# A recurrent attention kernel whose TensorE products are widened to 128 rows, and whose carry sum moves from VectorE to TensorE and ScalarE

## The chip, the cores and the metric

The kernel runs on one core of a Trainium2 chip. The core has five engines that run side by side, each with an instruction queue of its own that it works through in order: TensorE (PE in the profile, with its weight loads shown apart as PEld), VectorE (DVE), ScalarE (ACT), GpSimd (POOL) and SyncE (SP), which here only issues transfers. The metric is device time in microseconds (us) of one execution; lower is better. Three runs of the kernel before gave 1849.24, 1849.33 and 1851.26 us, a median of 1849.33 us.

## The reference

The computation has two parts. The first is a recurrence over 768 time steps for 4 batches of 8 heads, with a 40 x 40 state for each head:

```python
for t in range(S):
    kt, vt, rt = (k[:, :, t], v[:, :, t], r[:, :, t])
    wt, at, bt = (w[:, :, t], a[:, :, t], b[:, :, t])
    y[:, :, t] = np.einsum('bhd,bhde->bhe', rt, state)
    Sa = np.einsum('bhde,bhe->bhd', state, at)
    state_decay = state * wt[:, :, None, :] - np.einsum('bhd,bhe->bhde', Sa, bt)
    state = state_decay + np.einsum('bhd,bhe->bhde', vt, kt)
```

The second takes the 3072 x 320 output of the first as `x` and runs eight experts over it, `relu(x @ w1[e]) @ w2[e]` with 1024 hidden columns each, summed with gate weights `P` that come from `x @ w_gate` by an exponential and eight rounds of row and column normalisation. Everything is float32.

## The kernel before

**The recurrence in chunks.** `attention` cuts the 768 steps into 12 chunks of 64 steps (`NCH`, index `c`) and treats each of the 4 batches (`b`) as one unit, so there are 48 units (c, b). The 8 heads of a batch are held as 4 pairs (`NP`); a pair takes partitions 0 to 39 and 64 to 103, so that many tiles have 104 partitions (`R2`), the rows between being zero. All products of this part are float32; each call of `matmul` shows in the trace as two MATMUL instructions, each transpose as one.

**Preparation.** `prep(c, b)` (lines 106 to 169) needs only the inputs. It loads them, runs two scans on DVE (lines 113 and 123), scales the inputs (`kb` and `ab`, lines 137 to 144, on POOL for most units), multiplies them (`ll`, line 149, a 104-row product) and transposes `kb` (`kt`, line 157). Parts of the results go into the unit's `sx` and `bb` tiles by ScalarE copies (lines 145, 146, 164 to 166). A triangular inverse is needed for each chunk. It is made for two chunks at a time (`GROUPS`) on DVE by `inv_diag`, `contract` and `inv_off` (lines 171 to 198), and `tmat` (lines 223 to 237) finishes it with two sets of 64-row products, `gp` (line 230) and `op` (line 235).

**The recurrence of one unit.** `recur` (lines 239 to 312) is a chain over four engines:

1. `av` (line 259, TensorE, 104 rows) into PSUM, multiplied by a mask into `f` by DVE (line 260).
2. `xc[0]` and `xc[1]` (line 267, TensorE, 104 rows); ScalarE copies their upper part to `x1` (line 273) and their lower part to `c1` (line 274).
3. `pu` (line 278, TensorE, 128 rows, 104 columns for each pair), multiplied by a mask into `pm` by DVE (line 280).
4. `c2` (line 285, TensorE, 128 rows); DVE adds `c1` to it and writes `ws` (line 287).
5. POOL makes the output `y` (line 291) and then the carry `z` (line 302; DVE does it from chunk 9 on); TensorE transposes `z` (line 307) and ScalarE copies it (lines 309 and 310) for the unit of the same batch in the next chunk.

The PSUM tiles `av`, `xc`, `pu`, `c2` and `zt` share four buffers (tag `ps`). `f`, `rb` and `x1` are tiles of rotating pools; `vz` and `c1` are fixed buffers that are cleared once in `clear` (lines 81 to 87). `gate` (line 317) adds a product with 8 columns for each pair.

**Order.** An event list (lines 355 to 391) gives the order in which the units' steps are written down; the four batches are staggered by `SKEW`, and the preparation of chunk 2 and later and the inverses are interleaved with the recurrence. A list scheduler that works with a model of durations then fixes the order of instructions on each engine. From `N_MAN` = 8 blocks of the second part on, the order is the written one.

**The experts.** `body` (from line 439) runs the second part with products of 320 and 384 columns (lines 620 and 555) in the type `fp32r`, one MATMUL for each call. Its weights' preparation and its first blocks are mixed with the last chunks of the recurrence.

Of the kernel before, what the change touches and what calls it, by code (L numbers as in the profile page):

```python
# [29 lines left out]
def attention(ctx, tc, d, xd, ps, pq, pt, gs, lg):  # L30
    nc = tc.nc
    pin = ctx.enter_context(tc.tile_pool(name="a_in", bufs=1))
    inv = ctx.enter_context(tc.tile_pool(name="a_inv", bufs=1))
    sets = [ctx.enter_context(tc.tile_pool(name=f"a_set{i}", bufs=1)) for i in range(NSX)]
    const = ctx.enter_context(tc.tile_pool(name="a_const", bufs=1))
    io = ctx.enter_context(tc.tile_pool(name="a_io", bufs=1))
    wk = ctx.enter_context(tc.tile_pool(name="a_wk", bufs=2))
# [14 lines left out]
    for n in range(NCH * NB - NSX, NCH * NB):  # L52
        i, pool = n % NSX, sets[n - NCH * NB + NSX]
        if i in IN_SETS or i in KB_SETS:
            raw = pool.tile([128, 1252], F32, name=f"st{i}")
            raws[i] = raw
            sx_b[i] = raw[0:R2, 0:832].rearrange("r (p h x) -> r p h x", h=2, x=104)
            bb_b[i] = raw[:, 832:1248].rearrange("r (p x) -> r p x", x=104)
            cc_b[i] = raw[0:R2, 1248:1252]
            continue  # L60
        sx_b[i] = pool.tile([R2, NP, 2, 104], F32, name=f"sx{i}")
# [28 lines left out]
    def first_use(i):  # L90
        if i in fresh:
            fresh.discard(i)
            nc.gpsimd.memset(bb_b[i], 0.0)
            nc.scalar.copy(out=sx_b[i][64:R2].rearrange("r p h x -> r (p h) x")[:, :, 64:104],
                           in_=cst[64:R2, 360:400].unsqueeze(1).broadcast_to([40, 8, 40]))

    state = {"sx": 0, "ab": 0, "g1": 0, "vz": 0, "c1": 0, "t1": 0, "tt": 0}

    def rot(key, lst):
        i = state[key]  # L100
# [5 lines left out]
    def prep(c, b, ld):  # L106
# [38 lines left out]
        nc.scalar.copy(out=sx[64:104, :, 0, 0:64], in_=ab[0:40, :, 0:64])  # L145
        nc.scalar.copy(out=sx[64:104, :, 1, 0:64], in_=ab[64:104, :, 64:128])
        ll = pq.tile([128, NP, 2, 64], F32, name="ll", tag="pq")
        for p in range(NP):
            nc.tensor.matmul(ll[:, p], lhsT=kb[:, p], rhs=ab[:, p], start=True, stop=True)  # L149
        if cb < NKB:  # L150
            nc.scalar.activation(out=lt, in_=ll[64:128], func=AF.Copy, scale=-1.0)
            (nc.sync if cb < N_SP else nc.scalar).dma_start(out=ld[GRP[c][1], :, b], in_=lt)
# [2 lines left out]
            kt = pq.tile([128, NP, 2, 64], F32, name="kt", tag="pq")  # L155
        for p in range(NP):
            nc.tensor.transpose(kt[:, p].rearrange("s h x -> s (h x)")[:, 0:R2],
                                kb[:, p].rearrange("r k s -> r (k s)"), ident[0:R2, 0:R2])
# [43 lines left out]
    def tload(c):  # L202
        tt = rot("tt", tt_b)
        tts[c] = tt
        ld, ud, nd = invs[GRP[c][0]]
        t1, t2, lb = td_b[0][0:64], td_b[0][64:128], lg_b[0][0:64]
        cc = GRP[c][1]
        q = [slice(h * 32, h * 32 + 32) for h in range(2)]
        u = [[slice(cc * 64 + blk * 32 + h * 16, cc * 64 + blk * 32 + h * 16 + 16) for h in range(2)]
             for blk in range(2)]  # L210
        for h in range(2):
            nc.sync.dma_start(out=lb[q[h], :, q[h]],
                              in_=ld[cc, 0:32].rearrange("j b p h s -> j (b p) h s")[:, :, h, 32:64])
        for h in range(2):
            nc.sync.dma_start(out=t1[q[h]], in_=nd[u[0][h]].rearrange("g j s -> j g s"))
        for h in range(2):
            nc.sync.dma_start(out=t2[q[h]], in_=ud[u[1][h]].rearrange("g j s -> j g s"))
        for h in range(2):
            for blk in range(2):
                r = slice(h * 64 + blk * 32, h * 64 + blk * 32 + 32)  # L220
                nc.sync.dma_start(out=tt[r, :, r], in_=ud[u[blk][h]].rearrange("g j s -> j g s"))

    def tmat(c, half):
        gl = slice(half * 8, half * 8 + 8)
        tt = tts[c][:, gl]
        t1, t2 = td_b[0][0:64, gl], td_b[0][64:128, gl]
        lb, gs = lg_b[0][0:64, gl], lg_b[0][64:128, gl]
        gp = pt.tile([64, 2 * NP, 32], F32, name="gp", tag="pt")
        for p in range(2 * NP):
            nc.tensor.matmul(gp[:, p], lhsT=lb[:, p], rhs=t1[:, p], start=True, stop=True)  # L230
        nc.scalar.copy(out=gs[0:32, :, 0:32], in_=gp[0:32])
        nc.scalar.copy(out=gs[32:64, :, 32:64], in_=gp[32:64])
        op = pt.tile([64, 2 * NP, 32], F32, name="op", tag="pt")
        for p in range(2 * NP):
            nc.tensor.matmul(op[:, p], lhsT=gs[:, p], rhs=t2[:, p], start=True, stop=True)
        nc.scalar.copy(out=tt[0:32, :, 32:64], in_=op[0:32])
        nc.scalar.copy(out=tt[64:96, :, 96:128], in_=op[32:64])

    def recur(c, b):
        pp = preps[c, b]  # L240
        vz, zc = vz_cur[b], zp[b]
        nc.sync.dma_start(out=vz[:, :, 0:64], in_=d["v"][c, b])
        vz = vz[0:R2]
        rb = io.tile([RP, NP, 128], F32, name="rb", bufs=NRB)
        nc.sync.dma_start(out=rb, in_=d["r"][c, b])
        rb = rb[0:R2]
# [11 lines left out]
        for p in range(NP):  # L258
            nc.tensor.matmul(av[:, p], lhsT=vz[:, p], rhs=rb[:, p], start=True, stop=True)  # L259
        nc.vector.tensor_tensor(  # L260
            out=f[:, :, :, 0:64], in0=av,
            in1=mask_f.unsqueeze(1).unsqueeze(1).broadcast_to([R2, NP, 2, 64]), op=ALU.mult)
        yield
        xc = [ps.tile([R2, NP, 104], F32, name=f"xc{h}", tag="ps") for h in range(2)]
        for h in range(2):
            for p in range(NP):
                nc.tensor.matmul(xc[h][:, p], lhsT=pp["sx"][:, p, h], rhs=f[:, p, h], start=True, stop=True)  # L267
                if p % 2:
                    gate_step()
        x1 = wk.tile([128, NP, 104], F32, name="x1")  # L270
        c1 = rot("c1", c1_b)
        for h in range(2):
            nc.scalar.copy(out=x1[h * 64:h * 64 + 64], in_=xc[h][0:64])
            nc.scalar.copy(out=c1[h * 64:h * 64 + 40], in_=xc[h][64:104])
        yield
        pu = ps.tile([128, NP, 104], F32, name="pu", tag="ps")
        for p in range(NP):
            nc.tensor.matmul(pu[:, p], lhsT=tts[c][:, b * NP + p], rhs=x1[:, p], start=True, stop=True)  # L278
        pm = wk.tile([128, NP, 104], F32, name="pm")
        nc.vector.tensor_tensor(out=pm, in0=pu, in1=mask_p.unsqueeze(1).broadcast_to([128, NP, 104]),  # L280
                                op=ALU.mult)
        yield
        c2 = ps.tile([R2, NP, 104], F32, name="c2", tag="ps")
        for p in range(NP):
            nc.tensor.matmul(c2[:, p], lhsT=pp["bb"][:, p], rhs=pm[:, p], start=True, stop=True)  # L285
        ws = wk.tile([R2, NP, 104], F32, name="ws")
        nc.vector.tensor_tensor(out=ws, in0=c2, in1=c1, op=ALU.add)  # L287
# [523 lines left out]
```

## Time and profile before

| quantity | value |
|---|---|
| median of three runs | 1849.33 us (1849.24 to 1851.26) |
| the profiled execution | 1847.82 us |
| its span, first to last instruction | 1846.0 us |
| granted TensorE clock, mean over the span | 0.954 |
| ACT busy | 855.9 us (46%) |
| POOL busy | 873.1 us (47%) |
| SP: transfers of the input tile `inp` | 42, 450.2 KB each |

Durations in the text come from the one profiled execution, which took 1.8 us more than its span. "Busy" for PE is the time in which at least one MATMUL was under way. As these are pipelined, a product's duration in the trace (some 255 ns) is longer than the distance at which products follow each other. "PEclk" or "clock" is the share of the full TensorE clock that was granted. The chain of waits follows the work that ended last back from the end of the program, at each step to what released it. It gives shares of time by engine and line, and "issue" in it is time in which the engine waited for nothing that the profile shows.

### The profile page before, as it was taken

How to read it: one execution, taken by the hardware profiler on the slowest of the kernel's cores; microseconds unless marked ns; L12 is line 12 of the kernel's file. 1: busy time of each engine (PE TensorE's matmuls, PEld its weight loads, DVE VectorE, ACT ScalarE, POOL GpSimd, SP SyncE). 2: the span in 40 equal slices, each digit the busy share in tenths (PEclk: the TensorE clock that was granted, in tenths of full speed). 3: DMA queues.
4: the chain of work that ended last, by engine and by line, in shares of the span. 5: the costliest groups of instructions: out<-in, count | busy, mean ns of one | idle time of the engine just before them, and what ended most of it. 6: DMA issues, size and time to landing. Idle time of an engine off the chain costs nothing.

```text
span 1846.0 us, 31552 instructions
## 1 busy us (share of the span) xinstructions
PE 1734.9 (94%) x11843; PEld 1705.9 (92%) x11843; DVE 1397.2 (76%) x2306; ACT 855.9 (46%) x1848; POOL 873.1 (47%) x848
## 2 busy tenths in 40 slices
PE   5479898999989999999999999999999999999999
PEld 4378788899888999999999999999999999999999
DVE  7877969768698768677786868977686877778675
ACT  6347666666643534344343443445343443435342
POOL 6535556441572618355371826006291744628170
PEclk8569988889899999999999999999999999999999
DMA  8467787875720102011110202201020111102001
GB/s 211 116 152 177 184 183 181 182 173 133 203 82 31 56 1 75 20 56 38 38 56 19 75 20 67 65 14 57 19 75 19 57 38 38 57 19 75 5 34 43
DMA packets 194957, 145.10 MB, mean 79 GB/s; under 512 B 143861, under 2 KB 171637, under 8 KB 194805
## 3 DMA queue, kind: packets, MB, share of 16 engines
q1 hardware_dynamic: 191125, 137.35, 28.3%
q10 hardware_dynamic: 3680, 5.74, 1.1%
q8 instruction: 94, 1.54, 0.4%
q14 instruction: 58, 0.48, 0.1%
HBM read 117.00 MB, written 26.04 MB: 77 GB/s over the span
## 4 chain that ended last, share of the span: by engine, by line
PE 76%; DVE 10%; DMA 6%; issue 4%; ACT 2%; POOL 2%; SPq 1%; DVEq 0%; ACTq 0%; POOLq 0%
PE op L620 36%; PE p L555 33%; DMA inp<-in_inp_dram 2%; PE xc L267 2%; DVE pr L183 2%; DVE gt L186 1%; PE pu L278 1%; DVE q L113 1%; PE c L285 1%; PE av L259 1%; DVE un L186 1%; DMA ld<-lt 1%; DVE gf L123 1%; DMA rb<-in_r_dram 1%; DVE hl L579 1%
## 5 line engine op out<-in xcount | busy, mean ns | idle before, releaser
L555 PE MATMUL p<-xch,wh 128*128 128x384 f32 (+1 forms) x1792 | 605.7, 339 | 9.2 <-DVE sm L573 5.6
L576 ACT ACTIVATE hh<-sm 128x384 fp32r<-128x384 f32 x512 | 269.4, 526 | 726.4 <-DVE sm L573 726.2
L620 PE MATMUL op<-wh,hh 128*128 128x320 f32 x1536 | 476.8, 311 | 1.0 <-ACT hh L576 0.9
L620 PE MATMUL op<-wl,hh 128*128 128x320 f32 x1536 | 474.6, 309 | 0.0
L620 PE MATMUL op<-wh,hl 128*128 128x320 f32 x1536 | 467.1, 309 | 0.7 <-DVE hl L579 0.7
L501 POOL TENSOR_TENSOR wl<-ws,wh 128x640 fp32r<-128x640 f32 x60 | 103.6, 1727 | 608.5 <-ACT wh L499 608.3
L579 DVE SCALAR_TENSOR_TENSOR hl<-sm,hh 128x384 fp32r<-128x384 f32 x512 | 375.6, 767 | 2.4 <-ACT hh L576 2.0
L555 PEld LDWEIGHTS p<-xch,wh 128*128 128x128 f32 (+1 forms) x1792 | 337.4, 188 | 13.4 <-DVE sm L573 6.8
L555 PE MATMUL p<-xcl,wh 128*128 128x384 f32 x896 | 302.5, 338 | 0.0
L555 PE MATMUL p<-xch,wl 128*128 128x384 f32 x896 | 301.8, 337 | 0.0
L620 PEld LDWEIGHTS op<-wh,hh 128*128 128x128 f32 x1536 | 290.2, 189 | 1.6 <-ACT hh L576 1.5
L620 PEld LDWEIGHTS op<-wl,hh 128*128 128x128 f32 x1536 | 291.0, 189 | 0.0
L620 PEld LDWEIGHTS op<-wh,hl 128*128 128x128 f32 x1536 | 286.9, 188 | 1.1 <-DVE hl L579 0.9
L573 DVE TENSOR_TENSOR sm<-p,u 128x384 f32<-128x384 f32 x384 | 234.3, 621 | 8.8
L555 PEld LDWEIGHTS p<-xcl,wh 128*128 128x128 f32 x896 | 168.7, 188 | 0.0
L555 PEld LDWEIGHTS p<-xch,wl 128*128 128x128 f32 x896 | 168.6, 188 | 0.0
L573 DVE TENSOR_TENSOR sm<-p,p 128x384 f32<-128x384 f32 x128 | 71.2, 557 | 128.5 <-PE p L555 76.5
L573 DVE TENSOR_TENSOR p<-p,p 128x384 f32<-128x384 f32 x128 | 71.1, 555 | 98.7 <-PE p L555 98.0
L573 DVE TENSOR_TENSOR u<-p,p 128x384 f32<-128x384 f32 x128 | 70.8, 553 | 59.7 <-PE p L555 58.6
L509 POOL TENSOR_TENSOR wl<-ss,wh 128x512 fp32r<-128x512 f32 x60 | 89.9, 1498 | 32.7 <-ACT wh L506 28.4
L149 PE MATMUL ll<-ab,kb 104*128 104x128 f32 x336 | 64.0, 350 | 43.8 <-POOL ab L144 22.2
L291 POOL TENSOR_TENSOR y<-ws,gr 104x256 f32<-104x256 f32 x48 | 49.5, 1031 | 117.3 <-DVE ws L287 95.0
(156 smaller groups left out, 2774.4 us busy)
## 6 DMA issues: line engine op xcount, KB each, us to landing
ws<-in_wts_dram SPq DMA_DIRECT2D x60, 832.0 KB
inp<-in_inp_dram SPq DMA_DIRECT2D x42, 450.2 KB
rb<-in_r_dram SPq DMA_DIRECT2D x48, 224.0 KB
gd<-gf SPq DMA_DIRECT2D x48, 113.8 KB
gr<-gd SPq DMA_DIRECT2D x48, 113.8 KB
vz<-in_v_dram SPq DMA_DIRECT2D x48, 112.0 KB
ld<-lt ACTq DMA_DIRECT2D x40, 128.0 KB
f<-in_vt_dram SPq DMA_DIRECT2D x48, 80.0 KB
```

Source lines behind the costliest of these rows:

```text
L149: nc.tensor.matmul(ll[:, p], lhsT=kb[:, p], rhs=ab[:, p], start=True, stop=True)
L183: nc.vector.tensor_tensor(out=prv, in0=a.unsqueeze(3).broadcast_to([nu, n_c, n_k, n_r]), in1=m.unsqueeze(1).broadcast_to([nu, n_c, n_k, n_ ...
L186: nc.vector.tensor_reduce(out=dst, in_=prv.rearrange("u c k r -> u c r k"), op=ALU.add, axis=AX.X)
L267: nc.tensor.matmul(xc[h][:, p], lhsT=pp["sx"][:, p, h], rhs=f[:, p, h], start=True, stop=True)
L291: nc.gpsimd.tensor_tensor(out=y[:, :, b % 2], in0=ws[:, :, 0:64], in1=gr[0:R2, :, 64:0:-1], op=ALU.mult)
L501: g.tensor_tensor(out=wl[:, 0:640], in0=raw[:, 256:896], in1=wh[:, 0:640], op=ALU.subtract)
L509: g.tensor_tensor(out=lv[:, 3:7], in0=so[:, :, 0], in1=hv[:, 3:7, 0], op=ALU.subtract)
L555: nc.tensor.matmul(o, lhsT=w_, rhs=x_, start=(j == 0), stop=(j == 3))
L573: eng.tensor_tensor(out=out, in0=x, in1=y, op=ALU.add)
L576: nc.scalar.activation(out=hh[:, f, h], in_=sm[f][:, h], func=AF.Relu)
L579: v.scalar_tensor_tensor(out=hl[:, f, h], in0=sm[f][:, h], scalar=0.0, in1=hh[:, f, h], op0=ALU.max, op1=ALU.subtract)
L620: nc.tensor.matmul(ops[i], lhsT=a[:, h, cs], rhs=w_[:, cw], start=(f == 0 and h == 0 and j == 0), stop=(last and h == 1 and j == 2))
```

## The change

Two things are changed. First, products whose operands have 104 rows get operands with 128 rows: `sx`, `ab`, `kb`, `f`, `rb`, `vz` and `c1` become tiles of 128 partitions, of which the added rows are zero. `f`, `rb` and `x1` become fixed buffers that rotate, so that their zeros stay; new ScalarE instructions (`zero`) write these once. Products whose rows number 128 or 64 anyway get more columns instead: `pu` takes 128 columns for each pair in place of 104, and `gp` and `op` take 64 in place of 32, the second half of which is overwritten by the next product of the loop. `kt`, `zt` and the gate's products stay as they are, and so do the `ll` products of the first six units, whose `kb` lies in another tile.

Second, for chunks 0 to 7 (`CI` = 8) the sum of `c1` and `c2` is formed in PSUM. One more product, of the identity with `c1` (128 rows, 416 columns), starts the accumulation group, the four `bb` products add to it, and ScalarE copies the result to `ws`. From chunk 8 on DVE adds as before.

```diff
-            sx_b[i] = raw[0:R2, 0:832].rearrange("r (p h x) -> r p h x", h=2, x=104)
+            sx_b[i] = raw[:, 0:832].rearrange("r (p h x) -> r p h x", h=2, x=104)
...
-    td_b = [const.tile([128, 4 * NP, 32], F32, name="td")]
+    td_b = [const.tile([128, 4 * NP + 1, 32], F32, name="td")]
...
-    ab_b = [pin.tile([R2, NP, 128], F32, name=f"ab{i}") for i in range(2)]
+    ab_b = [pin.tile([128, NP, 128], F32, name=f"ab{i}") for i in range(2)]
+    kb1 = pin.tile([128, NP, 2, 64], F32, name="kb")
+    f_b = [const.tile([128, NP, 2, 104], F32, name=f"f{i}") for i in range(NFB)]
+    rb_b = [io.tile([128, NP, 128], F32, name=f"rb{i}") for i in range(NRB)]
+    x1_b = [const.tile([128, NP, 128], F32, name=f"x1{i}") for i in range(2)]
...
-    vz_b = [const.tile([RP, NP, 104], F32, name=f"vz{i}") for i in range(5)]
-    c1_b = [const.tile([R2, NP, 104], F32, name=f"c1{i}") for i in range(2)]
+    vz_b = [const.tile([128, NP, 104], F32, name=f"vz{i}") for i in range(5)]
+    c1_b = [const.tile([128, NP, 104], F32, name=f"c1{i}") for i in range(2)]
...
+    def zero(t):
+        src = cst[128 - t.shape[0]:128, 0:t.shape[1] * (t.shape[2] if len(t.shape) > 2 else 1)]
+        if len(t.shape) > 2:
+            src = src.rearrange("r (a b) -> r a b", b=t.shape[2])
+        nc.scalar.activation(out=t, in_=src, func=AF.Copy, scale=0.0)
...
+        for t, n in [(t[96:128], 512) for t in rb_b] + [(t[96:128], 832) for t in f_b] + [(kb1[96:128], 512)]:
+            r = t.rearrange("r a b -> r (a b)") if len(t.shape) == 3 else t.rearrange("r a b x -> r (a b x)")
+            zero(r[:, 0:n // 2])
+            zero(r[:, n // 2:n])
+        zero(td_b[0][:, 4 * NP])
+        for t in x1_b:
+            zero(t[:, :, 104:128])
...
-            nc.tensor.matmul(ll[:, p], lhsT=kb[:, p], rhs=ab[:, p], start=True, stop=True)
+            nc.tensor.matmul(ll[:, p], lhsT=kb[:, p], rhs=ab[0:kb.shape[0], p], start=True, stop=True)
...
-            nc.tensor.matmul(gp[:, p], lhsT=lb[:, p], rhs=t1[:, p], start=True, stop=True)
+            nc.tensor.matmul(gp[:, p:p + 2], lhsT=lb[:, p], rhs=t1[:, p:p + 2], start=True, stop=True)
...
-            nc.tensor.matmul(op[:, p], lhsT=gs[:, p], rhs=t2[:, p], start=True, stop=True)
+            nc.tensor.matmul(op[:, p:p + 2], lhsT=gs[:, p], rhs=t2[:, p:p + 2], start=True, stop=True)
...
-        pu = ps.tile([128, NP, 104], F32, name="pu", tag="ps")
+        pu = ps.tile([128, NP, 128], F32, name="pu", tag="ps")
...
         c2 = ps.tile([R2, NP, 104], F32, name="c2", tag="ps")
+        ws = wk.tile([R2, NP, 104], F32, name="ws")
+        if c < CI:
+            nc.tensor.matmul(c2, lhsT=ident[:, 0:R2], rhs=c1, start=True, stop=False)
         for p in range(NP):
-            nc.tensor.matmul(c2[:, p], lhsT=pp["bb"][:, p], rhs=pm[:, p], start=True, stop=True)
-        ws = wk.tile([R2, NP, 104], F32, name="ws")
-        nc.vector.tensor_tensor(out=ws, in0=c2, in1=c1, op=ALU.add)
+            nc.tensor.matmul(c2[:, p], lhsT=pp["bb"][:, p], rhs=pm[:, p], start=(c >= CI), stop=(c >= CI or p == NP - 1))
+        if c < CI:
+            nc.scalar.copy(out=ws, in_=c2)
+        else:
+            nc.vector.tensor_tensor(out=ws, in0=c2, in1=c1[0:R2], op=ALU.add)
```

More of the change, by code (lines that the diff above doesn't have):

```diff
@@ L60, in attention @@
             continue
-        sx_b[i] = pool.tile([R2, NP, 2, 104], F32, name=f"sx{i}")
+        sx_b[i] = pool.tile([128, NP, 2, 104], F32, name=f"sx{i}")
         bb_b[i] = pool.tile([128, NP, 104], F32, name=f"bb{i}")
@@ L93, in first_use @@
             nc.gpsimd.memset(bb_b[i], 0.0)
-            nc.scalar.copy(out=sx_b[i][64:R2].rearrange("r p h x -> r (p h) x")[:, :, 64:104],
-                           in_=cst[64:R2, 360:400].unsqueeze(1).broadcast_to([40, 8, 40]))
-    state = {"sx": 0, "ab": 0, "g1": 0, "vz": 0, "c1": 0, "t1": 0, "tt": 0}
+            nc.scalar.copy(out=sx_b[i][64:128].rearrange("r p h x -> r (p h) x")[:, :, 64:104],
+                           in_=cst[64:128, 360:400].unsqueeze(1).broadcast_to([64, 8, 40]))
+    state = {"sx": 0, "ab": 0, "g1": 0, "vz": 0, "c1": 0, "tt": 0, "f": 0, "rb": 0, "x1": 0}
     def rot(key, lst):
@@ L133, in prep @@
         else:
-            kb = pin.tile([R2, NP, 2, 64], F32, name="kb")
+            kb = kb1
             lt = pin.tile([64, NP, 2, 64], F32, name="lt")
@@ L137, in prep @@
         (nc.gpsimd if cb in KB_POOL else eng).tensor_tensor(
-            out=kb, in0=kb_in,
+            out=kb[0:R2], in0=kb_in,
             in1=q[:, :, 63::-1].unsqueeze(2).broadcast_to([R2, NP, 2, 64]), op=ALU.mult)
@@ L144, in prep @@
         eng.tensor_tensor(out=ab[64:104, :, 64:128], in0=a_in[64:104], in1=g[64:104], op=ALU.mult)
-        nc.scalar.copy(out=sx[64:104, :, 0, 0:64], in_=ab[0:40, :, 0:64])
-        nc.scalar.copy(out=sx[64:104, :, 1, 0:64], in_=ab[64:104, :, 64:128])
+        nc.scalar.copy(out=sx[64:128, :, 0, 0:64], in_=ab[0:64, :, 0:64])
+        nc.scalar.copy(out=sx[64:128, :, 1, 0:64], in_=ab[64:128, :, 64:128])
         ll = pq.tile([128, NP, 2, 64], F32, name="ll", tag="pq")
         for p in range(NP):
-            nc.tensor.matmul(ll[:, p], lhsT=kb[:, p], rhs=ab[:, p], start=True, stop=True)
+            nc.tensor.matmul(ll[:, p], lhsT=kb[:, p], rhs=ab[0:kb.shape[0], p], start=True, stop=True)
         if cb < NKB:
@@ L157, in prep @@
             nc.tensor.transpose(kt[:, p].rearrange("s h x -> s (h x)")[:, 0:R2],
-                                kb[:, p].rearrange("r k s -> r (k s)"), ident[0:R2, 0:R2])
+                                kb[0:R2, p].rearrange("r k s -> r (k s)"), ident[0:R2, 0:R2])
         nc.vector.tensor_tensor(
@@ L205, in tload @@
         ld, ud, nd = invs[GRP[c][0]]
-        t1, t2, lb = td_b[0][0:64], td_b[0][64:128], lg_b[0][0:64]
+        t1, t2, lb = td_b[0][0:64, 0:4 * NP], td_b[0][64:128, 0:4 * NP], lg_b[0][0:64]
         cc = GRP[c][1]
@@ L225, in tmat @@
         tt = tts[c][:, gl]
-        t1, t2 = td_b[0][0:64, gl], td_b[0][64:128, gl]
+        gw = slice(half * 8, half * 8 + 9)
+        t1, t2 = td_b[0][0:64, gw], td_b[0][64:128, gw]
         lb, gs = lg_b[0][0:64, gl], lg_b[0][64:128, gl]
-        gp = pt.tile([64, 2 * NP, 32], F32, name="gp", tag="pt")
+        gp = pt.tile([64, 2 * NP + 1, 32], F32, name="gp", tag="pt")
         for p in range(2 * NP):
[L230 to L233, printed above, removed]
+            nc.tensor.matmul(gp[:, p:p + 2], lhsT=lb[:, p], rhs=t1[:, p:p + 2], start=True, stop=True)
+        nc.scalar.copy(out=gs[0:32, :, 0:32], in_=gp[0:32, 0:2 * NP])
+        nc.scalar.copy(out=gs[32:64, :, 32:64], in_=gp[32:64, 0:2 * NP])
+        op = pt.tile([64, 2 * NP + 1, 32], F32, name="op", tag="pt")
         for p in range(2 * NP):
-            nc.tensor.matmul(op[:, p], lhsT=gs[:, p], rhs=t2[:, p], start=True, stop=True)
-        nc.scalar.copy(out=tt[0:32, :, 32:64], in_=op[0:32])
-        nc.scalar.copy(out=tt[64:96, :, 96:128], in_=op[32:64])
+            nc.tensor.matmul(op[:, p:p + 2], lhsT=gs[:, p], rhs=t2[:, p:p + 2], start=True, stop=True)
+        nc.scalar.copy(out=tt[0:32, :, 32:64], in_=op[0:32, 0:2 * NP])
+        nc.scalar.copy(out=tt[64:96, :, 96:128], in_=op[32:64, 0:2 * NP])
     def recur(c, b):
@@ L241, in recur @@
         vz, zc = vz_cur[b], zp[b]
[L242 to L246, printed above, removed]
+        nc.sync.dma_start(out=vz[0:RP, :, 0:64], in_=d["v"][c, b])
+        rb = rot("rb", rb_b)
+        nc.sync.dma_start(out=rb[0:RP], in_=d["r"][c, b])
         gr = io.tile([RP, NP, 65], F32, name="gr", bufs=NGR)
         nc.sync.dma_start(out=gr.rearrange("r p t -> r (p t)"), in_=gd[c, b])
-        f = wk.tile([R2, NP, 2, 104], F32, name="f", bufs=NFB)
+        f = rot("f", f_b)
         nc.sync.dma_start(out=f[0:64].rearrange("s p h x -> s (p h) x")[:, :, 64:104],
@@ L260, in recur @@
         nc.vector.tensor_tensor(
-            out=f[:, :, :, 0:64], in0=av,
+            out=f[0:R2, :, :, 0:64], in0=av,
             in1=mask_f.unsqueeze(1).unsqueeze(1).broadcast_to([R2, NP, 2, 64]), op=ALU.mult)
@@ L269, in recur @@
                     gate_step()
-        x1 = wk.tile([128, NP, 104], F32, name="x1")
+        x1 = rot("x1", x1_b)
         c1 = rot("c1", c1_b)
         for h in range(2):
-            nc.scalar.copy(out=x1[h * 64:h * 64 + 64], in_=xc[h][0:64])
+            nc.scalar.copy(out=x1[h * 64:h * 64 + 64, :, 0:104], in_=xc[h][0:64])
             nc.scalar.copy(out=c1[h * 64:h * 64 + 40], in_=xc[h][64:104])
         yield
-        pu = ps.tile([128, NP, 104], F32, name="pu", tag="ps")
+        pu = ps.tile([128, NP, 128], F32, name="pu", tag="ps")
         for p in range(NP):
@@ L406 @@
 NGR = 2
+CI = 8
 NFB = 3
```

2 lines of the change are left out of this document (1 added, 1 removed).

## The prediction

> **What bounds the kernel now.** I read the page first, its slices of PE and of the clock, then the busy time in three stretches.
>
> ```profile
> span 1846.0 us, 31552 instructions
> ...
> PE 1734.9 (94%) x11843; PEld 1705.9 (92%) x11843; DVE 1397.2 (76%) x2306; ACT 855.9 (46%) x1848; POOL 873.1 (47%) x848
> ...
> PEclk8569988889899999999999999999999999999999
> ...
> 138.00:405.00 267.00, 239.30 (x2195) 227.78 (x2194) 214.41 (x316) 183.54 (x464) 146.72 (x172) 0.91 0.78 181
> 405.00:505.00 100.00, 93.14 (x872) 88.61 (x871) 70.54 (x104) 63.34 (x151) 31.64 (x35) 0.90 0.68 167
> ...
> 600.00:1846.00 1246.00, 1240.02 (x7776) 1237.78 (x7774) 922.68 (x1577) 501.93 (x990) 570.06 (x491) 1.00 0.13 42
> ```
>
> The columns of a stretch are its length, then busy time and instructions of PE, PEld, DVE, ACT and POOL, then the granted clock, the DMA share and GB/s. From 600 us on, in the experts, PE is busy for 1240.0 of 1246 us at full clock. The change touches nothing there, so that part moves by whatever the recurrence gains or loses. The recurrence is where the clock falls to 0.9. Its chunks 0 to 7 end near 405 us; after that the preparation and the inverses are done. The chain of waits tells the two stretches apart:
>
> ```profile
> by line: issue 13.3%; DMA inp<-in_inp_dram 11.6%; DVE pr L183 7.1%; DVE gt L186 5.4%; DVE un L186 4.4%; DVE q L113 4.2%; DVE gf L123 3.5%; DMA ld<-lt 3.3%; PE xc L267 2.8%; PE ll L149 2.4%; DMA nd<-pr 2.3%; POOL y L291 2.2%; DVE pm L280 1.9
> ...
> by line: PE xc L267 16.8%; PE pu L278 10.9%; PE c L285 9.9%; PE av L259 9.7%; issue 7.0%; PE gp L230 5.7%; PE op L235 4.8%; PE lp L317 4.4%; PE p L555 4.2%; PE zt L307 4.0%; DMA ws<-in_wts_dram 3.6%; DVE xch L538 3.0%; DVE xcl L535 1.4%; DM
> ```
>
> The first row is 138 to 405 us: the DVE lines named add up to 26.5%, the two of PE to 5.2%. The second is 405 to 540 us: the PE lines add up to 70.4%. So DVE and transfers pace chunks 0 to 7, though PE is busy for 90% of the time there, and PE paces chunks 8 to 11.
>
> **The clock.** Asked in stretches of 3.41 us, it is either full or half:
>
> ```profile
> 272.79:276.20 3.41, 0.95 (x8) 1.00 0.55 109
> 276.20:279.61 3.41, 3.41 (x20) 0.50 0.70 167
> 279.61:283.03 3.42, 3.42 (x34) 1.00 0.89 217
> ...
> 122.60:132.84 10.24, 9.60 (x50) 0.50 0.81 168
> ...
> 535.61:539.02 3.41, 3.41 (x13) 0.50 0.00 0
> sum 81.90, PE 78.36; mean PE 6.53
> ...
> sum 23.88, PE 22.54; mean PE 5.64
> ```
>
> Here the columns after the length are PE, clock and DMA. PE had work for 0.95 us in one stretch, and the next ran at half clock, with 20 products in place of 34. From 120 us on there are twelve such dips, of which the first and the last are shown, 81.9 us long together; four of them, 23.9 us, lie behind 405 us. PE is busy for 78.4 us of the 81.9, so nearly all of a dip is paid in PE time at double price.
>
> What brings a dip on? Take the stretch from 361.53 (four rows, a dip follows) and the one from 286.44 (four rows, none follows), then those from 481.00 (three rows, half clock, full clock follows) and 364.94 (three rows, half clock, which stays):
>
> ```profile
> L278 PE MATMUL pu<-x,tt 128*128 128x104 f32 x8 | 1.1, 285 | 0.6 <-ACT c L274 0.6
> L235 PE MATMUL op<-td,lg 64*64 64x32 f32 x16 | 1.1, 220 | 0.0
> L317 PE MATMUL lp<-gs,y 104*128 104x8 f32 x8 | 1.1, 259 | 0.0
> L267 PE MATMUL xc<-f,sx 104*104 104x104 f32 x6 | 0.8, 272 | 0.0
> ...
> L278 PE MATMUL pu<-x,tt 128*128 128x104 f32 x8 | 1.1, 275 | 0.0
> L285 PE MATMUL c<-pm,st 128*104 128x104 f32 x8 | 0.9, 255 | 0.0
> L230 PE MATMUL gp<-td,lg 64*64 64x32 f32 x7 | 0.6, 219 | 0.0
> L307 PE MATMUL zt<-cst,z 104*40 104x104 f32 x4 | 0.5, 256 | 0.0
> ...
> L278 PE MATMUL pu<-x,tt 128*128 128x104 f32 x8 | 2.0, 436 | 0.0
> L267 PE MATMUL xc<-f,sx 104*104 104x104 f32 x8 | 1.5, 362 | 0.0
> L285 PE MATMUL c<-pm,bb 128*104 128x104 f32 x4 | 0.7, 304 | 0.0
> ...
> L149 PE MATMUL ll<-ab,kb 104*128 104x128 f32 x8 | 2.1, 441 | 0.1
> L267 PE MATMUL xc<-f,sx 104*104 104x104 f32 x6 | 1.1, 347 | 0.0
> L157 PE MATMUL kt<-cst,kb 104*128 104x104 f32 x4 | 0.9, 381 | 0.0
> ```
>
> By instructions the first had more work (38 against 27), and yet it lost the clock. By rows times streamed columns it had less: 8 x 128 x 104 + 16 x 64 x 32 + 8 x 104 x 8 + 6 x 104 x 104 = 211 thousand, against 271 thousand in the second. The other pair streams nearly the same columns, 2080 and 2064, but 246 against 215 thousand rows times columns, and only the former got the clock back. [...]
>
> [...]
>
> **The change part by part.** *Widened products.* The distances in time say what they cost:
>
> ```profile
> 442.83 1.63 PE L267 MATMUL xc<-f,st 104*104 104x104 f32 x16
> ...
> 444.68 1.10 PE L259 MATMUL av<-rb,vz 104*104 104x128 f32 x8
> ...
> 308.55 0.65 PE L230 MATMUL gp<-td,lg 64*64 64x32 f32 x8
> ...
> 310.24 1.06 PE L278 MATMUL pu<-x,tt 128*128 128x104 f32 x8
> ```
>
> Less the last product's own 0.25 us, an `xc` follows the one before by (1.63 - 0.255) / 15 = 0.092 us and a `pu` by 0.112, though both stream 104 columns: the 128 weight columns set `pu`'s distance. A `gp` takes 0.06 with 64 weight columns and 32 streamed. An `av`, with 128 streamed and 104 weight columns, takes 0.11. So `pu` with 128 and `gp`, `op` with 64 streamed columns should stay at the distance that their weights set: 0 us, and added rows 0 as well (`pu` with 128 rows is no slower per weight column than `av` with 104). Were the streaming added instead, 24 columns x 0.88 ns (0.092 / 104) x 384 `pu` would cost 8 us, and 32 x 0.88 ns x 768 `gp` and `op` 22 us, a bound that I find unlikely.
>
> Recounted with the new sizes, the 211 thousand become 283 and the 215 become 254: the first dip doesn't come, the second ends a stretch earlier. With the added product as well, the same count leaves 27.3 of the 81.9 us: four dips before 405 us (20.5 us) and those at 481 and 535 us (6.8 us), where PE stood nearly still beforehand. PE gets back half of the difference: 18.8 us before 405 us and 8.5 us behind it. Between 491 and 505 us the chain lies on PE nearly throughout, so I take 7 of the 8.5 us (bounds 0 and 12, all four dips).
>
> *The sum of c1 and c2.*
>
> ```profile
> L287 DVE TENSOR_TENSOR ws<-c,c 104x416 f32<-104x416 f32 x31 | 17.9, 577 | 9.1 <-PE c L285 8.3 <-ACT f L256 0.8
> L274 ACT COPY c<-xc 40x416 f32<-40x416 f32 x62 | 31.1, 502 | 3.0 <-DVE ws L287 1.8
> ```
>
> DVE loses 32 x 0.577 = 18.5 us. ACT gains 32 copies of 416 elements, 0.502 each, 16.1 us, which takes it from 69% to 75% of that stretch. Behind a copy that waits for `c2` stand the copies of the other batches, and `xc` and `pu` wait for those. PE gains an identity product that the trace doesn't have: two instructions of 416 columns. By `xc`'s 0.88 ns per column that is 0.73 us; by the experts, 1246 us / 7776 = 0.160 us for at most 384 columns, 0.35 us is the lower bound, and half clock, 1.47 us, the upper. I take 0.73, as the type is that of `xc`: 32 x 0.73 = 23.5 us (11 to 47). It needs `c1` alone, ready before `pm` is, so some of it fills a wait; but it takes a `ps` buffer, and PE works in order.
>
> Before 405 us: DVE and the issue gaps hold 39.8% of 267 us, 106 us; with 8.6% of DVE's 214 us gone, that is worth 9 us if nothing else ends last. PE's account is +23.5 - 18.8 = 4.7 us, which I charge whole, and ACT's I put at 1 (no ACT line reaches the chain row's last share, 1.9%, or 5 us). That leaves -3 us (bounds -12, and +16 from the rival below). A shorter wait for `ws` would make the next in line late: POOL's `y`, then `z`, and the `inp` transfers, which the change leaves as they are.
>
> *The start.*
>
> ```profile
> 4.58 4.39 ACT L94 COPY sx<-cst 40x320 f32<-40x320 f32 x12 [2.56 <-DMA cst<-in_cst_dram]
> 19.38 0.42 ACT L164 COPY sx<-kt 64x320 f32<-64x320 f32 x1 [4.21 <-PE kt L157]
> ...
> 5.42 0.59 SPq L245 DMA_DIRECT2D rb<-in_r_dram  x1
> ```
>
> Fifteen zeroing copies of at most 0.50 us, 6.6 us, join ACT, which is busy until 9 us and has a gap of 4.2 before 19.4 us. The first `rb` transfer, issued at 5.42, now waits for two of them, and behind it in SP's queue stand loads of the other units. I take +2 us (0 to 6.6).
>
> **The sum:** -7 - 3 + 2 = -8 us on the profiled execution's 1847.8, thus 1840; the runs' median lies 1.5 higher: 1841 us.
>
> **The rivals.**
>
> - *More comes of it.* DVE's 9 us come whole, PE's product hides in its waits, and all four dips behind 405 us go: -9 - 12 - 3 (the clock before 405 us), or 1825 us. For it speaks DVE's place in the chain, against it PE's 90%.
> - *It cancels.* The clock's 7 us come, but ACT's queue and the `ps` buffers give 7 back in chunks 0 to 7: 1849 us, within 0.2% (about 4 us, what a measurement can tell from no change).
> [...]
>
> **How the numbers follow.** Forecast 0.45 (1833 to 1846 alone), more 0.14, cancelling 0.17, slower 0.24: faster 0.59, same 0.17, slower 0.24. The range, 1826 to 1862 us, reaches nearly to the outer rivals' times. The scheduler's new order of instructions, which no row shows, can move each of them by some us.
>
> **What would show it.** Right: distances of `xc`, `pu`, `gp` unchanged; full clock behind 405 us but for one or two dips, and half-clock time from 120 us on near 27 us in place of 82; the identity's two instructions near 0.73 us; DVE's `ws` x16. Wrong: dips as long as before, `gp` or `pu` slower, PE over 95% busy in chunks 0 to 7 with waits for ACT's `ws`, or a late first `rb`.

## The result, and the profile after

| quantity | before | after |
|---|---|---|
| median of six runs each, us | 1850.99 (1849.24 to 1852.98) | 1860.85 (1858.56 to 1866.82) |
| ratio, 95% interval | | 1.0064 [1.0049, 1.0080] |
| profiled execution, us | 1847.82 | 1860.45 |

The change makes the kernel slower by 0.64%; forecast were 1841 us and faster. The first fence is the page of after, the same lines as shown of before.

```profile
span 1858.7 us, 31567 instructions
...
PE 1747.0 (94%) x11907; PEld 1703.4 (92%) x11907; DVE 1368.5 (74%) x2274; ACT 876.8 (47%) x1895; POOL 862.9 (46%) x848
...
PEclk8579999899899999999999999999999999999999
```

DVE has 32 instructions fewer and is busy for 28.7 us less, ACT is busy for 20.9 us more, and PE has 64 instructions more. In the slices of the clock the 8s behind the start are fewer. All of this is what the change meant, and yet the span is 12.7 us longer. To place these, both traces are cut where the 1st, the 32nd and the 48th `ws` are written: start, chunks 0 to 7, chunks 8 to 11. The columns are as in the prediction (length; busy time of PE, PEld, DVE, ACT, POOL; clock; DMA share; GB/s). First before, then after with the last 1246 us, the experts, in the fourth row:

```profile
0.00:127.20 127.20, 66.18 (x375) 59.92 (x376) 95.67 (x156) 59.94 (x148) 69.86 (x96) 0.65 0.69 163
127.20:409.40 282.20, 254.50 (x2316) 242.32 (x2315) 226.63 (x330) 192.66 (x486) 151.38 (x178) 0.91 0.77 178
409.40:520.00 110.60, 103.09 (x960) 98.38 (x959) 82.48 (x121) 68.44 (x160) 42.21 (x47) 0.91 0.63 158
```

```profile
0.00:123.30 123.30, 68.42 (x390) 62.43 (x390) 91.42 (x153) 65.37 (x164) 69.08 (x96) 0.67 0.69 165
123.30:422.30 299.00, 268.51 (x2364) 242.23 (x2363) 218.17 (x320) 207.65 (x517) 142.84 (x178) 0.94 0.74 171
422.30:532.70 110.40, 99.29 (x961) 93.52 (x960) 71.23 (x101) 68.24 (x161) 41.41 (x47) 0.95 0.62 152
612.70:1858.70 1246.00, 1239.92 (x7778) 1237.99 (x7776) 918.18 (x1577) 502.57 (x990) 569.94 (x491) 1.00 0.13 42
```

The start is 3.9 us shorter, chunks 0 to 7 take 16.8 us more, chunks 8 to 11 0.2 less: together +12.7, the whole of the difference. The experts are as before (1239.9 of 1246 us busy). So the loss lies in chunks 0 to 7, in which PE is busy for 14.0 us more and ACT for 15.0 more, while DVE has 8.5 less to do and is idle for 25 us more. Of the 18.5 us of additions only 8.5 are missing here, since the stage has but 10 DVE instructions fewer: steps of the preparation that ran outside it before now fall into it. A part of its growth is thus only where the cuts lie.

What the added instructions cost in place is in the groups and in the order of time (start, length, instructions) of after:

```profile
L302 PE MATMUL c<-c,cst 128*104 128x416 f32 x62 | 30.6, 578 | 3.7 <-ACT c L290 2.7 <-DVE pm L296 1.0
L306 ACT COPY ws<-c 104x416 f32<-104x416 f32 x31 | 15.7, 506 | 7.5 <-PE c L304 4.6 <-ACT lt L180 1.1 <-PE op L253 0.7
```

```profile
405.83 0.68 PE L248 MATMUL gp<-td,lg 64*64 64x64 f32 x9
406.44 0.94 PE L302 MATMUL c<-c,cst 128*104 128x416 f32 x2
407.23 0.89 PE L304 MATMUL c<-pm,bb 128*104 128x104 f32 x8
407.96 1.08 PE L294 MATMUL pu<-x,tt 128*128 128x128 f32 x8
408.87 1.63 PE L283 MATMUL xc<-f,sx 128*104 128x104 f32 x16
```

Eight `pu`, now with 128 columns, still take 1.08 us (1.06 before), sixteen `xc` with 128 rows still 1.63, and nine `gp` with 64 columns 0.68 (eight took 0.65). The second of the two identity instructions starts 0.94 - 0.578 = 0.36 us behind the first; the median over the trace is 0.353, so the product holds PE for 0.70 us, 22.6 us in 32 units.

And the waits of both kernels in this stage (who waited for whom: us in total, times, longest), before and then after:

```profile
POOL y L291 <- DVE ws L287: 50.1, 15, 9.3
POOL ab L143 <- DVE gf L123: 21.7, 9, 4.5
...
DVE q L113 <- DMA inp<-in_inp_dram: 14.0, 8, 3.6
POOL cc L142 <- DVE q L113: 11.7, 6, 2.8
...
DVE pm L280 <- PE pu L278: 3.6, 6, 1.6
```

```profile
POOL y L312 <- ACT ws L306: 44.2, 16, 7.3
POOL ab L160 <- DVE gf L140: 34.2, 16, 5.2
DVE q L130 <- DMA inp<-in_inp_dram: 27.6, 7, 5.0
...
POOL cc L159 <- DVE q L130: 22.1, 9, 4.5
...
DVE pm L296 <- PE pu L294: 13.6, 6, 3.7
```

POOL's wait for `ws` became 5.9 us shorter. But the preparation beside it waits longer at each link: DVE for the input 13.6 us more, POOL for DVE's two scans 12.5 and 10.4 more. In the recurrence DVE waits 10.0 us more for PE's `pu`. The time that DVE was relieved of has become waiting, for the next input and for PE.

### The profile page after: what moved, and what is told of

It reads as the page before. It is cut to its first block, busy times and chain, and to the rows that moved or that the text cites. A ratio compares the mean times of both kernels' runs of the same rounds, so it can differ in the third digit from the quotient of the medians.

```text
span 1858.7 us, 31567 instructions
## 1 busy us (share of the span) xinstructions
PE 1747.0 (94%) x11907; PEld 1703.4 (92%) x11907; DVE 1368.5 (74%) x2274; ACT 876.8 (47%) x1895; POOL 862.9 (46%) x848
## 4 chain that ended last, share of the span: by engine, by line
PE 75%; DVE 9%; issue 5%; POOL 3%; DMA 3%; ACT 1%; SPq 1%; POOLq 0%; DVEq 0%; ACTq 0%
PE op L642 35%; PE p L577 33%; PE xc L283 2%; DVE pr L200 1%; DMA inp<-in_inp_dram 1%; DVE gt L203 1%; POOL ab L160 1%; PE pu L294 1%; PE c L304 1%; PE av L275 1%; DVE un L203 1%; DVE q L130 1%; DMA ld<-lt 1%; PE ll L166 1%; DVE hl L601 1%
## 5 line engine op out<-in xcount | busy, mean ns | idle before, releaser
L601 DVE SCALAR_TENSOR_TENSOR hl<-sm,hh 128x384 fp32r<-128x384 f32 x512 | 371.7, 759 | 2.4 <-ACT hh L598 2.0
L166 PE MATMUL ll<-ab,kb 128*128 128x128 f32 x336 | 59.1, 329 | 50.2 <-POOL ab L161 24.5
L166 PEld LDWEIGHTS ll<-ab,kb 128*128 128x128 f32 x336 | 50.8, 230 | 55.2 <-POOL kb L154 28.0
```

The costliest lines, as they stand in the source:

```text
L166: nc.tensor.matmul(ll[:, p], lhsT=kb[:, p], rhs=ab[0:kb.shape[0], p], start=True, stop=True)
L601: v.scalar_tensor_tensor(out=hl[:, f, h], in0=sm[f][:, h], scalar=0.0, in1=hh[:, f, h], op0=ALU.max, op1=ALU.subtract)
```

## The experiments

Three theories stood against each other. A: the identity products cost the time, since PE is close to its bound in chunks 0 to 7. B: ScalarE costs it, since 32 more copies stand in an in-order queue ahead of copies that PE waits for. C: neither; any edit makes the list scheduler order the instructions anew, and before's order was a lucky one. Ratios are against runs of before on the same chip, with 95% intervals; 0.001 is 1.85 us. Rows of a trace come from the one profiled execution of a kernel, which can lie some us from the median of all its executions; ratios rest on all of them. "After" in a diff means that the edit starts from the changed kernel.

**The halves of the change.** Widening alone, from after:

```diff
-CI = 8
+CI = 0
```

> The widened products without the sum in PSUM: DVE adds c1 to c2 in all chunks, as in the kernel before. Theory A (the identity products fill TensorE: 64 instructions at a distance of 0.35 us are 22.6 us more on an engine that was busy for 90% of chunks 0 to 7): the gain of the widening shows here, 5 to 15 us below the kernel before, near 1840 us. Theory B (ScalarE's copies of the sum come late in its queue): the same, near 1840. Theory C (the scheduler's new order of instructions costs more than the operations themselves): near 1855 to 1861, for the order changes here too. Under A and B half-clock time from 118 us on is 40 to 55 us, against 87 before.

The sum alone, in before:

```diff
+        nc.tensor.matmul(c2, lhsT=ident[0:R2, 0:R2], rhs=c1, start=True, stop=False)
...
-        nc.vector.tensor_tensor(out=ws, in0=c2, in1=c1, op=ALU.add)
+        nc.scalar.copy(out=ws, in_=c2)
```

> The sum in PSUM and ScalarE's copy, with the products as narrow as before. Theory A: slower than the changed kernel, 1865 to 1872 us, since TensorE gets the added products without the clock time that the widening gives back. Theory B: near 1865, by the copies. Theory C: anywhere from 1850 to 1870. The dips of the clock tell whether the wide added product alone keeps the clock up: by a count of rows times columns half-clock time falls from 87 to some 55 us.

After without the identity product, ScalarE's copy kept:

```diff
-            nc.tensor.matmul(c2, lhsT=ident[:, 0:R2], rhs=c1, start=True, stop=False)
```

> The changed kernel without the identity products: in chunks 0 to 7 ScalarE copies c2 alone to ws, and the sum with c1 is left out. Theory A: the 22.6 us on TensorE go, and the time falls to 1836 to 1845 us. Theory B: it stays near 1861, since ScalarE's copies are all there. Theory C: no forecast, 1845 to 1861.

After with VectorE copying in place of ScalarE:

```diff
-            nc.scalar.copy(out=ws, in_=c2)
+            nc.vector.tensor_copy(out=ws, in_=c2)
```

> The changed kernel with the identity products, but DVE instead of ScalarE copies the sum out of PSUM in chunks 0 to 7. Theory A: 1861 us or more, up to 1870, since DVE has its 32 instructions back and TensorE keeps the added products. Theory B: it falls to 1845 to 1852, since ScalarE is rid of its 16 us. Theory C: no forecast.

| kernel | median us | ratio |
|---|---|---|
| widening alone | 1845.46 | 0.9991 [0.9971, 1.0011] |
| the sum alone | 1868.46 | 1.0120 [1.0091, 1.0149] |
| after, no identity product | 1845.69 | 0.9989 [0.9975, 1.0004] |
| after, VectorE copies | 1854.95 | 1.0041 [1.0023, 1.0059] |

The loss is in the sum, and within it in the product: without it the kernel stands where widening alone does. Against B alone: with VectorE copying, 7.5 us of loss remain. With the product in it, the widening gives 10 us back (ratios 1.0120 and 1.0064). In the narrow kernel the sum costs 0.0120 or 22 us and hardly any clock comes back with it, against the expectation: the mean granted clock of all executions is 0.952, as in before.

As forecasts these runs were poor for all three theories. A and B put the widening alone 5 to 15 us below before, and it is 2 below; C put it at 1855 us or more. A put after without the product at 1836 to 1845 us, nearly where it came out, but the time with VectorE's copy lies between A's and B's.

**Each part's price.** The product alone: wide, the identity product made and then overwritten, VectorE adds as in before (from after):

```diff
-            nc.tensor.matmul(c2, lhsT=ident[:, 0:R2], rhs=c1, start=True, stop=False)
+            nc.tensor.matmul(c2, lhsT=ident[:, 0:R2], rhs=c1, start=True, stop=True)
...
+        nc.vector.tensor_tensor(out=ws, in0=c2, in1=c1[0:R2], op=ALU.add)
```

> The widened products, and the identity product at its place in TensorE's order, but its sum is overwritten by the bb products and DVE adds c1 in all chunks: 22.6 us more on TensorE than the kernel with the widening alone, all else alike. Theory A: 12 to 22 us more than that kernel's 1845, thus 1857 to 1867. Theory B: within 4 us of it, 1845 to 1849. If TensorE and ScalarE share the blame: 1850 to 1856.

After with a shorter product (`c1` and the identity in `fp32r`, one instruction in place of two):

```diff
-            nc.tensor.matmul(c2, lhsT=ident[:, 0:R2], rhs=c1, start=True, stop=False)
+            nc.tensor.matmul(c2, lhsT=identr, rhs=c1, start=True, stop=False)
```

> The changed kernel with the identity product in the type fp32r (c1 and the identity are written as fp32r): one instruction of 416 columns, some 0.19 us in place of 0.70, so 16 of its 22.6 us on TensorE go. Theory A: the loss falls to a quarter or a third, 1847 to 1851. Theory B: 1856 to 1861, since ScalarE's copies are unchanged.

Before with a second VectorE addition for chunks 0 to 7, and before with a ScalarE copy ahead of VectorE's addition:

```diff
+            nc.vector.tensor_tensor(out=more, in0=c2, in1=c1, op=ALU.add)
```

> The kernel before, with the DVE addition of c2 and c1 made a second time for every unit of chunks 0 to 7, into a tile that nobody reads: 32 instructions, some 18.5 us more on DVE. If DVE paces these chunks, as the chain of waits was read for the prediction, the time rises by 9 to 18 us. If it doesn't (theory A, TensorE), by 0 to 4 us.

```diff
+            nc.scalar.copy(out=more, in_=c2)
```

> The kernel before, with one more ScalarE copy of c2 (416 elements) for every unit of chunks 0 to 7, into a tile that nobody reads: some 16 us more on ScalarE. Theory A (TensorE paces): 0 to 4 us more. Theory B (ScalarE's queue is what the added copies lengthen): 5 to 15 us more.

| kernel | median us | ratio |
|---|---|---|
| wide, product alone | 1856.51 | 1.0041 [1.0024, 1.0059] |
| after, product in `fp32r` | 1852.10 | 1.0020 [1.0006, 1.0034] |
| before, VectorE adds twice | 1866.10 | 1.0111 [1.0067, 1.0154] |
| before, ScalarE copies too | 1865.24 | 1.0076 [1.0052, 1.0101] |

The product alone costs 1.0041 - 0.9991 = 0.0050 or 9 us more than widening, and ScalarE's copy in VectorE's place a further 0.0023 or 4 us, at the edge of the intervals; together they are after's 1.0064. Chunks 0 to 7 of the product alone, and of widening alone:

```profile
124.80:419.80 295.00, 267.29 (x2376) 240.56 (x2377) 238.36 (x353) 191.97 (x486) 151.49 (x178) 0.95 0.76 173
```

```profile
122.90:409.60 286.70, 255.41 (x2320) 241.41 (x2319) 232.56 (x339) 192.86 (x486) 156.41 (x178) 0.91 0.75 177
```

The clock records of before and after hold the values 1.00 and 0.50 alone; taken so for every kernel, the time at half clock is length x (1 - clock) x 2: about 30 us of 295.0 here and 52 of 286.7 there. Half of such time is counted as lost to PE, an estimate from before's trace, in which the stretches of 3.41 us with PE busy throughout hold some 20 products at half clock (276.20 us, 481.00 us) and 34 to 41 at full clock (279.61, 306.91, 484.41 us). So the product brings 22.6 us of work, and 22 us less at half clock give by that count some 11 us of PE's time back; PE is busy for 11.9 us more and the stage grows by 8.3. Some three quarters of PE's account are charged. Theory A had put the product at 12 to 22 us. The shorter product, with 16 us less of PE's time by its expectation, agrees: 0.0044 or 8 us less, though PE also orders its work anew. Adding work to DVE or to ACT costs about what it lasts as well: by the ratios 20 us (12 to 28) for 18.5 us of additions, and 14 us (10 to 19) for 16 us of copies. The first is about what the chain of waits foretold (9 to 18 us), and theory A alone, with 0 to 4 us for either, doesn't explain them. But neither is clean, as the first reads `c2` a second time, for 0.578 us, and the second stands between `c2` and `ws` (DVE's `ws` waited 9.1 us for it in all), and both lost clock: over all executions its mean is 0.942 in each, against 0.950 in the runs of before beside them, or 17 and 16 us of PE's time, nearly all of the loss. Whether the added work was paid on its own engine or through PE's clock isn't settled by these two. In the profiled execution of the second, the slowest of its five, it shows most:

```profile
118.00:545.00 427.00, 391.83 (x3353) 373.02 (x3352) 319.55 (x472) 283.03 (x693) 195.95 (x230) 0.85 0.70 163
```

That is some 128 us at half clock, where before, in the same stretch, has some 85:

```profile
118.00:545.00 427.00, 383.87 (x3423) 365.02 (x3424) 341.55 (x496) 279.03 (x681) 215.93 (x245) 0.90 0.70 167
```

**Is the relief of VectorE worth anything?** Three kernels in which one of the four pairs is summed or copied in chunks 0 to 7: wide with a short addition on VectorE, wide with a short copy on ScalarE, and after with a short copy.

```diff
+            nc.vector.tensor_tensor(out=ws[:, 0], in0=c2[:, 0], in1=c1[0:R2, 0], op=ALU.add)
```

> The widened products without the identity product; in chunks 0 to 7 DVE adds c1 to c2 for one of the four head pairs alone (the other three pairs are left out of ws), so that every wait stays and DVE gets about 12 us back, with nothing put on ScalarE. If relief of DVE is worth its time in these chunks, as the prediction reckoned (9 us for 18.5), 6 to 12 us below the widening alone (1845), thus 1833 to 1839. If ScalarE's added copies merely gave it back in the kernel without the product, this shows it. If DVE doesn't pace: 1842 to 1846.

```diff
+            nc.scalar.copy(out=ws[:, 0], in_=c2[:, 0])
```

> The widened products without the identity product; in chunks 0 to 7 ScalarE copies one of the four pairs of c2 to ws (the sum with c1 and the other three pairs are left out): DVE has its 18.5 us back and ScalarE gets some 8 us in place of 16. If both engines' queues count: 1833 to 1840. If neither does (TensorE and the order pace): 1842 to 1846, as with the whole copy.

```diff
-            nc.scalar.copy(out=ws, in_=c2)
+            nc.scalar.copy(out=ws[:, 0], in_=c2[:, 0])
```

> The changed kernel with its identity products, but in chunks 0 to 7 ScalarE copies one pair of the sum alone (three pairs are left out of ws): some 8 us less on ScalarE. If the copy's length on ScalarE is part of the loss: 4 to 8 us below the changed kernel, 1849 to 1854 beside a before of 1848. If TensorE's products are all of it: within 3 us of the changed kernel, which stands 12 us above before, thus 1857 to 1862.

And the product, overwritten, in chunks 8 to 11 alone, in the wide kernel:

```diff
-        if c < CI:
-            nc.tensor.matmul(c2, lhsT=ident[:, 0:R2], rhs=c1, start=True, stop=False)
+        if c >= CI:
+            nc.tensor.matmul(c2, lhsT=ident[:, 0:R2], rhs=c1, start=True, stop=True)
```

> The widened products with the identity product in chunks 8 to 11 instead of 0 to 7, its sum overwritten, DVE adding in all chunks: 16 x 0.70 = 11.3 us more on TensorE where the chain of waits lay on it. Theory A with the stages as the chain shows them: 8 to 11 us above the widening alone (1845), 1853 to 1856, a full price for each product, against 9 us for 22.6 in chunks 0 to 7. If a product costs the same share everywhere: 1849 to 1851.

| kernel | median us | ratio |
|---|---|---|
| wide, short addition | 1839.94 | 0.9948 [0.9928, 0.9967] |
| wide, short copy | 1844.56 | 0.9978 [0.9964, 0.9992] |
| after, short copy | 1868.60 | 1.0105 [1.0083, 1.0127] |
| wide, product in chunks 8 to 11 | 1858.37 | 1.0051 [1.0034, 1.0069] |

The short addition's row, of chunks 0 to 7, shows what DVE is relieved of:

```profile
L305 DVE TENSOR_TENSOR ws<-c,c 104x104 f32<-104x104 f32 x32 | 8.0, 251 | 9.5 <-PE c L303 4.8 <-ACT vz L330 2.4 <-ACT bb L184 1.3
```

18.5 - 8.0 = 10.5 us less on DVE are worth 0.9991 - 0.9948 or 8 us (3 to 13 by the intervals), in this one order: the relief has a value. With the whole 18.5 us taken off DVE and 16.2 put on ACT instead (after without the product) nothing is left of it, 0.9989 against 0.9991. Chunks 0 to 7 of that kernel:

```profile
123.10:409.40 286.30, 250.01 (x2305) 234.23 (x2304) 219.61 (x313) 208.71 (x519) 160.08 (x178) 0.94 0.78 178
```

Against widening alone DVE is busy for 13 us less and some 17 us less are spent at half clock, and the stage is 0.4 us shorter: neither saving reaches its end. This execution was the slowest of its twelve, 6 us above their median, so that the row alone would show little; the ratio, of all twelve, shows the same. Cutting the copy to a quarter of its width saves only 2 us more, which is within the intervals. So ACT's part is not its length alone; that it is the instruction's place in ACT's queue is argued, not shown. The short copy in after was a miss for every theory: less work, and 8 us slower than after. It fits no price of a part; that it is the changed order is argued. It shows that differences between two orders cannot be read to better than some 8 us, the relief's 8 and the copies' 4 among them. The product in chunks 8 to 11, whose stage is shown first for that kernel and then for widening alone,

```profile
409.00:530.80 121.80, 113.56 (x992) 101.72 (x991) 80.74 (x114) 68.32 (x160) 43.73 (x47) 0.94 0.58 143
```

```profile
409.60:518.70 109.10, 97.00 (x948) 91.19 (x947) 76.41 (x114) 68.17 (x160) 43.84 (x47) 0.97 0.65 160
```

made it 12.7 us longer for 16 x 0.70 = 11.3 us of work and about 8 us more at half clock, or 4 us of PE time counted by half: there PE's time is paid nearly in full. By the ratios, too, the product costs 11 us there, 0.0060 more than widening alone.

**How much is the order's luck?** One number of the event list, the time at which the preparation of later chunks enters it, was moved by 0.1 of a step both ways, in before, in the wide kernel and in after. The instructions remain the same; their order changes.

```diff
-P0 = -8
+P0 = -8.1
```

> The kernel before with P0 = -8.1 in place of -8: the same instructions on the same data, but preparations are written down a tenth of an event step earlier, and the scheduler comes to another order on every engine. If the order is worth little: within 4 us of before. If the order moves the time by as much as the changed parts do: 4 to 15 us off, either way.

> The kernel before with P0 = -7.9: as the run with -8.1, the other way. Within 4 us of before, or 4 to 15 us off if the order counts.

> The changed kernel with P0 = -8.1. If the loss of 12 us belongs to the operations (TensorE's products, ScalarE's queue), it stays 8 to 16 us above before. If it belongs to this one order of instructions, it can be anywhere from 4 us below before to 25 above.

> The changed kernel with P0 = -7.9. The same two cases: 8 to 16 us above before, or anywhere from -4 to +25. The mean over the three orders of the changed kernel, against the mean over the three of the kernel before, is what the change itself is worth.

> The widened products alone with P0 = -8.1. The kernel before stood 8 us higher in this order than in its own. If the widening is worth the 2 us that one order showed: 1852 to 1858 beside a before of 1848.5. If it is worth the clock time that it gives back at half to full price, 5 to 10 us: 1845 to 1852.

> The widened products alone with P0 = -7.9, where before stood 6 us higher than in its own order: 1850 to 1856 if the widening is worth 2 us, 1843 to 1850 if it is worth 5 to 10.

| order | before | widening alone | after |
|---|---|---|---|
| -8 | 1 | 0.9991 [0.9971, 1.0011] | 1.0064 [1.0049, 1.0080] |
| -8.1 | 1.0045 [1.0031, 1.0059] | 0.9988 [0.9977, 0.9999] | 1.0078 [1.0062, 1.0094] |
| -7.9 | 1.0032 [1.0011, 1.0053] | 0.9979 [0.9966, 0.9991] | 1.0065 [1.0050, 1.0080] |
| mean | 1.0026 | 0.9986 | 1.0069 |

C holds in part. Before's order was the best of its three, by 6 to 8 us, and an edit loses that. But in each order after is the slowest, and the wide kernel level with before or faster. By the means, widening is worth -0.40% (-7 us), the sum +0.83% (+15 us), the change as a whole +0.43% (+8 us). Of the 12 us measured in the first order, the remaining 4 are the order's: before stands 5 us below its own mean there, and after 1 us below its own. The sum costs 0.7, 0.9 and 0.9% in the three orders. The widening's gain is 0.1, 0.6 and 0.5%, the first of which is within noise. Three orders are few, and the means may be off by 0.1 to 0.2%.

The best complete version is the wide kernel: 1843.23 us in the last order, 0.9979 [0.9966, 0.9991], 4 us below before.

## Why the prediction was wrong

**The step that failed** is the second, the sum of `c1` and `c2`, put at -3 us. By the means over three orders it is +15, by the kernels in the first order +13: 9 us for the product and 4 for the copies in VectorE's place. Its terms were mis-sized, all in the same direction.

- *DVE's relief -9 and ACT's copies +1*, together -8. This is the larger miss. The relief is worth about that much when the work goes nowhere (8 us for 10.5). Moved to ACT it is worth nothing without the product, and with it the copies cost 4 us more than VectorE's addition, at the edge of the intervals. ACT's place outside the chain's first rows said what ACT costs now, not what 32 more instructions would cost in front of the copies for `xc` and `pu`. That this place in the queue is the reason stays open.
- *PE, put at +4.7 us.* The product was right, 22.6 us for 23.5. The clock that should have paid for it was not: 18.8 us were to come back before 405 us, and the time at half clock in chunks 0 to 7 fell from 53.4 to 34.1 us only (the stage's rows, rounded to hundredths of the clock, give 51 and 36), or 9.6 us of PE's time counted by half. PE's account is then +22.6 - 9.6 = +13 us, and PE is busy for 14.0 us more; the kernels say that some 9 us of it reach the time. The count was made on before's trace with the products enlarged where they stood, and left four dips of 20.5 us before 405 us. From which sum of rows times columns on a dip goes is shown by no run, nor are the 27.3 us left and the 18.8 and 8.5 us of PE's time worked out from them: they were the author's estimate. In the new order the dips lie in other places: there are eight in chunks 0 to 7, 34.1 us long together, and one of 10.2 us in chunks 8 to 11. That the product's time is really charged is shown by the product alone (+9 us) and by the shorter one (-8 us).

**The widened products** were right in price: sixteen `xc` take 1.63 us as before, eight `pu` 1.08 for 1.06, nine `gp` 0.68 for 0.65 of eight. Their worth, -7 us by the means, is the figure of the forecast, but that is luck. The forecast's -7 stood for the clock behind 405 us alone, and in the profiled order chunks 8 to 11 are 0.2 us shorter, not 7, though the time at half clock there fell from 20 to 11 us (rows of the stages). The clock did come back: by its mean over all executions, 0.961, 0.964 and 0.963 against 0.952, 0.948 and 0.948, widening alone gains some 17, 30 and 28 us of PE's time on before in the orders -8, -8.1 and -7.9. But only 2, 11 and 10 us of these reach the end. Over the whole stretch of 427 us the clock of after is 0.95, some 43 us at half clock, where 27 were foretold and before had some 85:

```profile
118.00:545.00 427.00, 383.44 (x3434) 350.05 (x3432) 305.73 (x444) 287.78 (x700) 195.64 (x235) 0.95 0.70 164
```

**The start**, put at +2, came out at -3.9 us, although the zeroing copies are there and the first `rb` transfer does wait for them:

```profile
6.39 1.33 ACT L89 ACTIVATE rb<-cst 32x256 f32<-32x256 f32 x4
7.62 2.72 ACT L89 ACTIVATE f<-cst 32x416 f32<-32x416 f32 x6
```

```profile
8.33 2.67 SPq L262 DMA_DIRECT2D rb<-in_r_dram  x2
```

It is issued at 8.33 in place of 5.42 us, and the stage ends no later for it. Where the 3.9 us come from wasn't tried; the wide kernel has them too (122.9 against 127.2 us), and loses them again in chunks 0 to 7 (286.7 against 282.2), so part of it is only where the cut falls.

**The rivals.** Slower had a chance of 0.24, and 1860.85 us lies 1 us inside the range's upper end. The bound of +16 us for the sum is shown by no run: chunks 0 to 7 grew by 16.8 us in the profiled execution, part of it by where the cuts lie, and by the ratios the product costs 9 us and the copies 4. In the rival by which more comes of it, PE's product hides in PE's waits and DVE's relief comes whole; instead the product was charged, and the relief was lost with ACT's copies. The rival by which it cancels had the widening right by the means, -7 us, but the sum gave back 15, not 7. PE is busy for 268.51 of 299 us, 90% as before, although the product was added and the dips became fewer. Why the share stays is argued only: the preparation, whose steps stand in the same queues, grows longer with the stage (the waits shown behind the result). A busy share of 90% can be taken as room of 10%; the added work found little of it.

## What to carry to other kernels

Here three engines, busy for some 70 to 90% of chunks 0 to 7, hand work to each other in order, and work moved between them was not credited at the relieved engine's place in the chain and charged at the other's. In such a case price the added work at up to its whole time (here 9 us for 22.6 in one stage, 11 for 11.3 in the other), and the relief at nothing until a kernel that merely leaves that work out shows its worth. A count of dips made on the old trace did not hold in the new order (20.5 us foretold, 34.1 measured). When a scheduler orders anew on each edit, time the kernel in two or three neighbouring orders, before and after, ahead of believing half a per cent.

## What the runs showed of the hardware

**The clock was either full or half.** The clock records of before and after have two values, 1.00 and 0.50. The dips of chunks 0 to 7 in after last 3.41 or 6.83 us each, the one in chunks 8 to 11 10.24 us.

**With the widened products the mean clock was higher.** Widening alone has a mean clock over all executions of 0.961, 0.964 and 0.963 in the orders -8, -8.1 and -7.9, before in the same orders 0.952, 0.948 and 0.948. Whether this comes from the products with more rows, which are zeros, or from those with more columns, no run separates. That the clock follows rows times columns was the author's reading of four stretches of before: 211 thousand ahead of a dip and 271 ahead of none, 215 where half clock stayed and 246 where it ended; no run shows it beyond these. The added rows cost PE no time here (sixteen `xc` take 1.63 us with 104 rows and with 128), and the widening gained 0.4% of the time, by the mean over three orders.

**Another order of the same instructions lost clock.** Before in the order of -8.1 has the instructions of before, and more time at half clock:

```profile
118.00:545.00 427.00, 383.10 (x3388) 364.90 (x3386) 328.94 (x482) 275.40 (x674) 210.08 (x238) 0.88 0.71 166
```

About 17 us more at half clock are 8.5 us of PE time counted by half, and that order is 0.45% or 8 us slower; over all executions its mean clock is 0.948, against 0.950 in the runs of before beside them. The ScalarE copy ahead of VectorE's addition took the time at half clock from some 85 to some 128 us. What PE waits for ahead of these dips wasn't traced.
